# SwiGLU feed-forward on one core: the transposing load of tokens 256-511 goes from SyncE's queue to ScalarE's, and the first up weights the other way

## The chip, the core and the metric

The kernel runs on one core of a Trainium2 chip. The metric is the device time of one execution in microseconds (us), lower is better. The core has five engines with a queue of instructions each: TensorE (PE in the profile; PEld is its weight loader), VectorE (DVE), ScalarE (ACT), GpSimd (POOL) and SyncE (SP). SyncE only issues transfers here. Transfers that SyncE and ScalarE issue are moved by the same 16 DMA engines.

## The reference

```python
B, S, D, F = 1, 2048, 512, 1376
# x: (1, S, D); w_gate, w_up: (D, F); w_down: (F, D); all bf16

def reference(x, w_gate, w_up, w_down):
    g = _silu(x @ w_gate)
    u = x @ w_up
    return (g * u) @ w_down
```

## The kernel before, in words

**Stages.** TensorE contracts over the partitions, so x is needed transposed: `xT_sb` holds D in four blocks of 128 partitions, tokens along the free side. The 2048 tokens make four chunks of 512 (`c`), the 1376 columns of F ten blocks of 128 (`ft`) and 96 more. First stage: for each chunk and each `ft` a gate group and an up group, each of four matmuls (one for every block of D) into a PSUM bank; ScalarE applies SiLU to the gate bank, VectorE multiplies it with the up bank into `hT_sb`. The last 96 columns are made in groups X and Y. Second stage: the 16 token tiles times the down weights; VectorE copies each out (ScalarE one piece), SyncE stores it.

**The order of the first chunk.** The order of TensorE's work is written out by hand. It starts with eight matmuls on ones (`warm`, L337), which need no data. Then it waits for tokens 0-255, which are loaded as they lie (`xn_sb`, load "xn"), and transposes them itself: eight transposes into four banks (L346), two for each half of the tokens and each half of D. VectorE copies the two banks of D's first half to `xT_sb` (L293), ScalarE those of the second half (L280). Tokens 256-511 come by a transposing DMA instead (load "x0b", `load_x`, L87), as do tokens 512 to 2047 (x1, x2, x3).

So as not to wait for x0b, TensorE takes the first two gate and up groups in halves (L349-356): gate 0, up 0, gate 1, up 1 for tokens 0-255 first, then all four for tokens 256-511. Each waits, by `need`, for its own weights ("wg0", "wu0", "wg1", "wu1") and for the copies it reads; the second halves wait for x0b. From `ft` 2 on, a group has one matmul of 512 tokens for each block of D.

**Loads.** `load_w` (L91) brings a slab of columns of one weight; the slabs are block 0, block 1, blocks 2-3, 4-6, and 7 on. ScalarE issues gate 0 and up 0 (L104); behind these, in its own queue, come the table load with a dummy SiLU (L269), then the copies and SiLUs in the order of TensorE's groups (L270-280). SyncE issues all else (L107): xn, gate 1, up 1, x0b, the later slabs, the up tail ("wut"), x1 to x3, the down weights, and then it waits for each finished tile and stores it. In every queue the instructions run in order: an issue that takes long holds what stands behind it.

Of the kernel before, what the change touches and what calls it, by code (L numbers as in the profile page):

```python
# [13 lines left out]
def bass_standalone__swiglu_ffn__prompt_kernel(nc, x, w_gate, w_up, w_down, out):  # L14
    _, S, D = x.shape
    F = w_gate.shape[1]
    P = 128
# [4 lines left out]
    SC = 512  # L22
# [6 lines left out]
    HT = SC // 2  # L29
# [10 lines left out]
    UPH = F + 32  # L40
# [4 lines left out]
    with ExitStack() as es:  # L45
# [29 lines left out]
        loads = {}  # L75

        def load_sem(name):
            loads[name] = sem(f"s_{name}")
            return loads[name]
# [6 lines left out]
        def load_x(eng, name, t0, t1):  # L86
            eng.dma_start_transpose(  # L87
                xT_sb[:, :, t0:t1], xf[t0:t1, :]
            ).then_inc(load_sem(name), 16)

        def load_w(eng, name, src, base, f0, f1):  # L91
            eng.dma_start(
                w_sb[:, :, base + f0:base + f1],
                src[:, f0:f1].rearrange("(k p) f -> p k f", p=P),
            ).then_inc(load_sem(name), 16)

        slabs = [(0, 1), (1, 2), (2, 4), (4, 7), (7, NFT)]
        slab_of = {ft: a for a, b in slabs for ft in range(a, b)}

        def load_slab(eng, a, b):  # L100
            load_w(eng, f"wg{a}", w_gate, 0, a * P, min(b * P, F))
            load_w(eng, f"wu{a}", w_up, UPH, a * P, min(b * P, F - 32))

        def loads_on_scalar(act):  # L104
            load_slab(act, *slabs[0])

        def loads_on_sync(sp):  # L107
            sp.dma_start(
                xn_sb[:, :, :].rearrange("p j d -> p (j d)"), xf[0:HT, :].rearrange("(p j) d -> p (j d)", j=NXN)
            ).then_inc(load_sem("xn"), 16)  # L110
            load_slab(sp, *slabs[1])
            load_x(sp, "x0b", HT, SC)
            for a, b in slabs[2:]:
                load_slab(sp, a, b)
            load_w(sp, "wut", w_up, F - (F - 32), F - 32, F)
            for c in range(1, NSC):
                load_x(sp, f"x{c}", c * SC, (c + 1) * SC)
            sp.dma_start(
                wd_sb[:, 0:NFF, :], w_down[0:NFF * P, :].rearrange("(k p) d -> p k d", p=P)
            ).then_inc(load_sem("wd"), 16)  # L120
            for c in range(NSC):
                sp.dma_start(
                    wdt_sb[R * c:R * (c + 1), :, :], w_down[NFF * P:F, :].rearrange("(q p) d -> p q d", p=R)
                ).then_inc(load_sem(f"wdt{c}"), 16)
            sp.dma_start(wdl_sb[:, :], w_down[NFF * P:F, LASTA:D]).then_inc(load_sem("wdl"), 16)
# [123 lines left out]
        def rows_of(t):  # L249
            if t < NXN:  # L250
                return of[0:HT, :].rearrange("(p j) d -> j p d", j=NXN)[t]
            return of[t * P:(t + 1) * P, :]

        def on_sync(sp):
            loads_on_sync(sp)
            for t, c0, c1, ob, eng, n in stores:
                sp.wait_ge(s_A if eng == "A" else s_D, n)
                sp.dma_start(rows_of(t)[:, c0:c1], o_sb[ob][:, c0:c1]).then_inc(s_out[ob], 16)
            for i in range(NOS):
                sp.wait_ge(s_out[i], 16 * n_store[i])  # L260

        def on_gpsimd(pool):
            pool.iota(
                diag[:, :], pattern=[[-1, P]], base=0, channel_multiplier=1,
            ).then_inc(s_I, 1)

        def on_scalar(act):
            loads_on_scalar(act)
            act.activation(adummy[:, 0:4], zero_c, ACT.Silu)  # L269
            for op in act_ops:  # L270
                act.wait_ge(s_P, op["g"]["at"] + 1)
                if op["kind"] == "silu":
                    if op["free"]:
                        act.wait_ge(s_D, op["free"])
                    fn = ACT.Silu
                else:
                    if op["stored"][1]:
                        act.wait_ge(*op["stored"])
                    fn = ACT.Copy
                act.activation(op["out"], op["src"], fn).then_inc(s_A, 1)  # L280
# [15 lines left out]
        def on_tensor(pe):  # L296
# [136 lines left out]
                skip_group_check=True,  # L433
            ).then_inc(s_P, 1)

        on_sync(nc.sync)
        on_gpsimd(nc.gpsimd)
        on_scalar(nc.scalar)
        on_tensor(nc.tensor)
        on_vector(nc.vector)  # L440

# [27 lines left out]
```

## Time and profile before

| what | value |
|---|---|
| median of 3 runs | 120.66 us (120.31, 120.93, 120.66) |
| the profiled execution | 120.32 us; its span, first to last instruction, 118.9 us |
| granted TensorE clock | 1.00 |
| issue of x0b on SyncE | at 2.21 us, takes 1.69 us, landed at 6.38 us |
| issue of up 0 on ScalarE | at 1.22 us, takes 0.53 us, landed at 4.88 us |
| issues of x1, x2, x3 on SyncE | 4.54, 2.98, 1.80 us, from 8.86 us on |

The page of the profile gives busy times, the span in 40 slices of 3.0 us, the DMA queues, the chain of work that ended last, the costliest groups of instructions by line, and the transfers. Beside it stand answers of the trace: a timeline, the waits, the landings. In such lines "L87" is a line of the kernel, "out<-in" its tensors, "ACTq" and "SPq" the queues of ScalarE and SyncE while they issue a transfer, "x2" how many instructions; "[0.94 <-PE bank L346]" is idle time before and what ended it. All times in a timeline count from the first instruction of the span.

### The profile page before, as it was taken

How to read it: one execution, taken by the hardware profiler on the slowest of the kernel's cores; microseconds unless marked ns; L12 is line 12 of the kernel's file. 1: busy time of each engine (PE TensorE's matmuls, PEld its weight loads, DVE VectorE, ACT ScalarE, POOL GpSimd, SP SyncE). 2: the span in 40 equal slices, each digit the busy share in tenths (PEclk: the TensorE clock that was granted, in tenths of full speed). 3: DMA queues.
4: the chain of work that ended last, by engine and by line, in shares of the span. 5: the costliest groups of instructions: out<-in, count | busy, mean ns of one | idle time of the engine just before them, and what ended most of it. 6: DMA issues, size and time to landing. Idle time of an engine off the chain costs nothing.

```text
span 118.9 us, 1519 instructions
## 1 busy us (share of the span) xinstructions
PE 115.4 (97%) x600; PEld 54.1 (45%) x611; DVE 47.3 (40%) x73; ACT 31.0 (26%) x53; POOL 0.4 (0%) x5
## 2 busy tenths in 40 slices
PE   7999999999999999999999999999999999999993
PEld 2774444444444444444444444344434444444452
DVE  0133443353443444433444334469617422006530
ACT  4344324454234363244262343230000000000001
POOL 1000000000000000000000000000000000000000
PEclk9999999999999999999999999999999999999999
DMA  3999999970000000000000000000004221002412
GB/s 103 271 307 357 264 162 242 328 183 24 0 0 0 6 0 0 0 3 3 0 0 0 6 0 0 0 0 0 0 0 138 88 88 44 0 0 75 145 50 88
DMA packets 17559, 8.84 MB, mean 74 GB/s; under 512 B 10640, under 2 KB 17424, under 8 KB 17552
## 3 DMA queue, kind: packets, MB, share of 16 engines
q1 hardware_dynamic: 16496, 8.48, 26.7%
q10 hardware_dynamic: 1056, 0.26, 1.0%
q8 instruction: 5, 0.08, 0.3%
q14 instruction: 2, 0.02, 0.1%
HBM read 4.81 MB, written 2.10 MB: 58 GB/s over the span
## 4 chain that ended last, share of the span: by engine, by line
PE 97%; issue 1%; DVE 0%
PE bank L328 58%; PE bank L394 29%; PE bank L370 3%; PE bank L337 2%; PE bank L408 2%; PE bank L381 2%; PE bank L346 1%; DVE o_sb L293 0%; PE bank L431 0%
## 5 line engine op out<-in xcount | busy, mean ns | idle before, releaser
L328 PE MATMUL bank<-xT_sb,w_sb 128*128 128x512 bf16 (+2 forms) x338 | 69.7, 364 | 0.4
L328 PEld LDWEIGHTS bank<-xT_sb,w_sb 128*128 128x128 bf16 x344 | 32.8, 98 | 36.4 <-issue 0.2
L289 DVE TENSOR_TENSOR hT_sb<-sg_sb,bank 128x512 bf16<-128x512 f32 x40 | 27.5, 688 | 40.5 <-PE bank L328 36.6
L394 PE MATMUL bank<-wd_sb,hT_sb 128*128 128x512 bf16 (+2 forms) x166 | 34.5, 366 | 0.4 <-issue 0.3
L280 ACT ACTIVATE sg_sb<-bank 128x512 f32<-128x512 f32 x40 | 23.8, 596 | 40.8 <-PE bank L328 40.8
L394 PEld LDWEIGHTS bank<-wd_sb,hT_sb 128*128 128x128 bf16 x170 | 16.1, 98 | 19.1 <-issue 1.3
L293 DVE CAST o_sb<-bank 128x512 bf16<-128x512 f32 (+1 forms) x16 | 10.1, 663 | 22.0 <-PE bank L408 12.3
L280 ACT ACTIVATE o_sb<-bank 128x384 bf16<-128x384 f32 x1 | 0.5, 492 | 37.8 <-PE bank L394 37.8
L289 DVE TENSOR_TENSOR ht_sb<-sgy_sb,bank 32x512 bf16<-32x512 f32 x8 | 5.5, 684 | 0.2
L289 DVE TENSOR_TENSOR ht_sb<-sgx_sb,bank 32x512 bf16<-32x512 f32 x4 | 2.8, 691 | 3.5 <-ACT sgx_sb L280 3.5
L370 PE MATMUL bank<-xT_sb,w_sb 128*128 128x512 bf16 x15 | 4.1, 379 | 0.1
L337 PE MATMUL bank<-const-bfloat16-1.0 128*128 128x512 bf16 (+1 forms) x8 | 2.9, 545 | 0.8 <-PEq L454 0.8
L280 ACT ACTIVATE sgx_sb<-bank 32x512 f32<-32x512 f32 x4 | 2.4, 588 | 4.5 <-PE bank L370 4.5
L408 PE MATMUL bank<-wdt_sb,ht_sb 32*128 32x512 bf16 (+1 forms) x48 | 2.9, 372 | 0.0
L370 PEld LDWEIGHTS bank<-xT_sb,w_sb 128*128 128x128 bf16 x16 | 1.6, 98 | 1.9
L280 ACT ACTIVATE sgy_sb<-bank 64x512 f32<-64x512 f32 x4 | 2.4, 590 | 0.1
L337 PEld LDWEIGHTS bank<-const-bfloat16-1.0 128*128 128x128 bf16 x8 | 1.0, 136 | 2.4 <-issue 2.4
L381 PE MATMUL bank<-xT_sb,w_sb 128*64 128x512 bf16 x16 | 1.9, 382 | 0.0
L408 PEld LDWEIGHTS bank<-wdt_sb,ht_sb 32*128 32x128 bf16 x48 | 1.1, 93 | 1.7 <-issue 0.8
L269 ACT ACT_TABLE_LOAD x1 | 1.3, 1283 | 1.8 <-issue 1.8
L293 DVE COPY xT_sb<-bank 128x256 bf16<-128x256 bf16 x2 | 0.6, 292 | 2.7 <-PE bank L346 2.7
L381 PEld LDWEIGHTS bank<-xT_sb,w_sb 128*64 128x64 bf16 x16 | 0.8, 109 | 1.0 <-DVE hT_sb L289 0.4
(14 smaller groups left out, 4.0 us busy)
## 6 DMA issues: line engine op xcount, KB each, us to landing
out_dram<-o_sb SPq DMA_DIRECT2D x15, 128.0 KB, 1.7
wd_sb<-in_w_down_dram SPq DMA_DIRECT2D x1, 1280.0 KB, 9.2
w_sb<-in_w_gate_dram SPq DMA_DIRECT2D x1, 480.0 KB, 5.9
w_sb<-in_w_up_dram SPq DMA_DIRECT2D x1, 448.0 KB, 6.5
w_sb<-in_w_gate_dram SPq DMA_DIRECT2D x1, 384.0 KB, 4.5
w_sb<-in_w_up_dram SPq DMA_DIRECT2D x1, 384.0 KB, 5.1
wdt_sb<-in_w_down_dram SPq DMA_DIRECT2D x4, 96.0 KB, 7.5
xn_sb<-in_x_dram SPq DMA_DIRECT2D x1, 256.0 KB, 2.8
```

What stands on the lines that cost most here:

```text
L269: act.activation(adummy[:, 0:4], zero_c, ACT.Silu)
L280: act.activation(op["out"], op["src"], fn).then_inc(s_A, 1)
L289: ins = dve.tensor_tensor(op["out"], op["a"], op["b"], ALU.mult)
L293: ins = dve.tensor_copy(op["out"], op["src"])
L328: ins = pe.matmul(g["bank"][:, n0:n1], lhsT=w_sb[:, dk, col:col + P], rhs=xT_sb[:, dk, c * SC + n0:c * SC + n1], start=(dk == 0), stop=(dk ...
L337: pe.matmul(banks[NB - 1][:, 0:width], lhsT=ones_w, rhs=ones_m[:, 0:width], start=True, stop=True)
L346: ins = pe.transpose(tview(g["bank"])[:, k, :], xn_sb[:, g["i"], dk * P:(dk + 1) * P], ident[:, :])
L370: ins = pe.matmul(g["bank"][:, :], lhsT=w_sb[:, dk, XC0:XC0 + P], rhs=xT_sb[:, dk, c * SC:(c + 1) * SC], start=(dk == 0), stop=(dk == KD - 1),
L381: ins = pe.matmul(g["bank"][y0:y1, :], lhsT=w_sb[:, dk, YC0:YC0 + 64], rhs=xT_sb[:, dk, c * SC:(c + 1) * SC], start=(dk == 0), stop=(dk == ...
L394: ins = pe.matmul(g["bank"][:, 0:c1 - c0], lhsT=hT_sb[:, fk, t * P:(t + 1) * P], rhs=wd_sb[:, fk, c0:c1], start=(start and fk == 0), stop= ...
L408: ins = pe.matmul(g["bank"][:, 0:c1 - c0], lhsT=ht_sb[R * c:R * (c + 1), q, j * P:(j + 1) * P], rhs=wdt_sb[R * c:R * (c + 1), q, c0:c1], s ...
```

## The change

ScalarE issues gate 0 and then x0b, the transposing load. SyncE issues xn, then up 0, gate 1, up 1 and the later slabs, each in the place that is now free, and x0b is no longer among them. Ahead of x1, the first transposing load that SyncE still has, it waits until x0b has landed, so that transposing loads of the two queues are never in flight together. The last hunk only has ScalarE's instructions emitted ahead of SyncE's, since the semaphore of x0b is made where x0b is issued.

```diff
         def loads_on_scalar(act):
-            load_slab(act, *slabs[0])
+            load_w(act, "wg0", w_gate, 0, 0, P)
+            load_x(act, "x0b", HT, SC)
 
         def loads_on_sync(sp):
             sp.dma_start(
                 xn_sb[:, :, :].rearrange("p j d -> p (j d)"), xf[0:HT, :].rearrange("(p j) d -> p (j d)", j=NXN)
             ).then_inc(load_sem("xn"), 16)
+            load_w(sp, "wu0", w_up, UPH, 0, P)
             load_slab(sp, *slabs[1])
-            load_x(sp, "x0b", HT, SC)
             for a, b in slabs[2:]:
                 load_slab(sp, a, b)
             load_w(sp, "wut", w_up, F - (F - 32), F - 32, F)
+            sp.wait_ge(loads["x0b"], 16)
             for c in range(1, NSC):
                 load_x(sp, f"x{c}", c * SC, (c + 1) * SC)
...
+        on_scalar(nc.scalar)
         on_sync(nc.sync)
         on_gpsimd(nc.gpsimd)
-        on_scalar(nc.scalar)
         on_tensor(nc.tensor)
         on_vector(nc.vector)
```

## The prediction

> **What bounds the kernel now.** First the busy times and the slices (page, parts 1 and 2).
>
> ```profile
> PE 115.4 (97%) x600; PEld 54.1 (45%) x611; DVE 47.3 (40%) x73; ACT 31.0 (26%) x53; POOL 0.4 (0%) x5
> ...
> DMA  3999999970000000000000000000004221002412
> ```
>
> TensorE is busy for 115.4 us of the 118.9 us span; the transfers fill the first quarter only. A change that touches loads can move the time only where TensorE waits for a load. So second the chain of waits, in order of time (start, duration, what), at its beginning:
>
> ```profile
> 0.77 2.93 PE bank L337 x8
> 3.71 0.70 PE bank L346 x8
> 4.41 0.07 issue
> 4.47 3.87 PE bank L328 x40
> 8.35 0.05 issue
> 8.40 10.74 PE bank L328 x49
> ```
>
> L337 are the matmuls on ones that fill the wait for x, L346 the eight TensorE transposes of tokens 0-255, L328 the gate and up matmuls. From 4.47 us on the chain is matmul after matmul. Whatever the change brings is decided before about 8.4 us; only the loads needed there count. Third the waits between 4 and 9 us (total, times, longest):
>
> ```profile
> ACT xT_sb L280 <- PE bank L346: 0.9, 1, 0.9
> PEld bank L328 <- issue: 0.2, 1, 0.2
> PEld bank L328 <- DMA xT_sb<-in_x_dram: 0.2, 1, 0.2
> ```
>
> The load that moves, the transposing load of tokens 256-511 ("x0b" below), is the only load that TensorE is seen to wait for, 0.17 us by its weight loader. The matmul row shows less: the last first-half matmul starts at 6.266 us and its successors follow 0.109 us apart, so the next was due at 6.375 and came at 6.426: **0.05 us**. That is all that this wait can give back. ScalarE meanwhile waits 0.9 us before its first copy of transposed x. Fourth, the timeline at the start (start, duration):
>
> ```profile
> 1.22 0.53 ACTq L92 DMA_DIRECT2D w_sb<-in_w_up_dram  x1
> ...
> 1.78 1.28 ACT L269 ACT_TABLE_LOAD   x1 [1.78 <-issue]
> 2.20 1.69 SPq L87 DMA_TRANSPOSE xT_sb<-in_x_dram  x1
> ...
> 3.08 0.20 ACT L269 ACTIVATE act_dummy<-const-float32-0.0 128x4 f32<-128x4 f32 x1
> ...
> 4.22 0.66 ACT L280 ACTIVATE xT_sb<-bank 128x256 bf16<-128x256 bf16 x2 [0.94 <-PE bank L346]
> ```
>
> The transposing load holds its issuing engine for 1.69 us, an ordinary load for about 0.5. And ScalarE, on which it now goes, has its table load, its dummy SiLU and the copies of L280 behind its loads.
>
> **Part 1: ScalarE's order.** Removed there: issue of up 0, 0.531 us from 1.223. Added there: issue of x0b, of unknown length d on this engine. Nearest row: the same load on SyncE, 1.690. Lower end: the load of tokens 1536-2047 has twice the tokens and took 1.795, so half of it is 0.90. Upper end: that of tokens 512-1023, behind a full queue, took 4.537. I take 1.69, same size and same neighbours. Then: 1.223 + 1.690 = 2.913 issue done; + 0.03 gap + 1.283 table load = 4.23; + 0.01 + 0.205 dummy = 4.44; the first copy starts near **4.46** in place of 4.221. The cover is the 0.9 us wait above, and it ends at d = 1.47 (2.75 + d = 4.22). In other words 1.16 us of added hold lie against 0.92 us of cover, and **0.24 us** show. TensorE is behind it at once: its third matmul waits for this copy now too (second at 4.530, third at 4.660 instead of 4.586), and four matmuls later for the second copy (0.04 us late). Both copies shift together, so the delay counts once: +0.24. VectorE's copies (4.04, 4.33) do not move.
>
> The Trainium skill, page "ScalarE: Activation LUTs", section "What ACT_TABLE_LOAD costs", adds a drain of about 1.38 us to the 1.283 us of the load itself. The trace shows no such drain: the dummy starts 0.01 us behind the load. With it the copies would be 1.38 us later still, about 122.3 us for the median; I give that 1 in 100, within the slow rival below.
>
> **Part 2: the transfers.** Landings now, issue plus time to landing (page, part 6):
>
> ```profile
> xn_sb<-in_x_dram SPq DMA_DIRECT2D x1, 256.0 KB, 2.8
> ...
> w_sb<-in_w_gate_dram ACTq DMA_DIRECT2D x1, 128.0 KB, 3.2
> w_sb<-in_w_gate_dram SPq DMA_DIRECT2D x1, 128.0 KB, 3.4
> w_sb<-in_w_up_dram ACTq DMA_DIRECT2D x1, 128.0 KB, 3.7
> w_sb<-in_w_up_dram SPq DMA_DIRECT2D x1, 128.0 KB, 3.7
> ```
>
> x lands at 3.50, gate 0 at 3.93 (needed at 4.44), gate 1 at 4.58 (5.45), up 0 at 4.88 (5.00), up 1 at 5.33 (5.83), x0b at 6.38 (6.37). All but x move as packets of 256 B: 512 for each weight, 1024 for x0b. By the trace's packet records the DMA engines are full from 2 us on (share 0.96 or more in each stretch to 6.5 us), and between 3.5 and 5.5 us start 2218 such packets, 1109 a us; the last of the 3072 starts near 5.75. While both queues had packets (3.5 to 4.5 us) SyncE's moved 596 and ScalarE's 517: about half each.
>
> After the change gate 0 and x are as before, since the second load of each queue stands behind its first: x lands at 3.5, gate 0 at 3.9. At 3.5 us x0b follows gate 0 in ScalarE's queue, and SyncE's has up 0 (383 packets left), gate 1, up 1. At 555 packets a us each, up 0 ends at 4.19, gate 1 at 5.11 with 129 of x0b left, x0b at 5.34, up 1 at 5.69. From last packet to landing the trace has 0.4 to 0.5 us for weights (0.48 gate 1, 0.55 up 1) and 0.62 for x0b. So up 0 lands near 4.6 (earlier than now), gate 1 at 5.6 (needed at 5.45 + 0.24 = 5.69), x0b at 5.96, and **up 1 at 6.24**, needed at 5.83 + 0.24 = 6.07. Up 1 takes x0b's place as the late load: its four half-width matmuls run from about 6.29 to 6.73, where the second halves now start at 6.43: +0.30. If SyncE's queue is served first, up 1 is in time and the end of Part 1 alone counts: 6.375 + 0.24 = 6.615, or +0.19. Part 1 lies inside Part 2's delay, they do not add.
>
> What speaks against any gain here is a rule of the Trainium skill, "DMA: Bandwidth & Descriptors", section "Issuing engines are not separate DMA queues": loads from several engines share the same 16 DMA engines, and a second issuer saves only issue time. By it up 1 is late as worked out (+0.30); if x0b had engines of its own, the +0.19 would remain. The packet counts above side with the rule.
>
> **Part 3: the rest of SyncE's queue.** Later weights are issued 1.2 us earlier, but their packets stand behind the same 3072 as before, so gate 2-3 still lands near 7.2, needed at 8.08 + 0.25: no cost. The new wait on x0b comes on SyncE after the up tail (7 issues at about 0.55 from 2.75, then 1.44: near 7.5 us); x0b has landed at 5.96, so it does not hold. Queued behind it are the loads of tokens 512 on, the down weights and the stores. Tokens 512-1023 land at 17.0 now and are needed at 23.0: 6 us of cover, and if the wait held, it would have to hold that long to cost anything. Emitting ScalarE's program ahead of SyncE's moves no instruction on any engine: 0.
>
> **Sum.** +0.19 to +0.30; I take +0.25. Against the profiled execution (120.32, span 118.9 and 1.4 around it) 120.57; that run is at the low end of the three shown, so against their median of 120.66 I forecast **120.91 us**. Half a per cent, 0.6 us, is about what a measurement of this kernel can tell from no change: this is no change.
>
> **Rivals.**
> *x0b was the late load more often than the profile shows.* It has no slack now, and the runs shown spread from 120.31 to 120.93; if the upper ones wait longer for it, a landing at 5.96 takes that wait away. With d under 1.47 and SyncE's queue served first, this gives -0.05 in the profiled run and up to -0.35 in the median: 120.3 to 120.6. For it: the lower end of d, 0.90. Against: the full DMA engines. Chance 0.17, of which 0.05 under 120.06.
> *Slower: ScalarE is held longer.* The place is the first copy at L280; it pays from d = 1.47, us for us, and passes half a per cent at d near 2.1. With the 2.976 us that the load of tokens 1024-1535 held SyncE, it is 0.24 + 1.29 - 0.05 = +1.5, or 122.1. For it: two of four such loads took that or more. Against: those stood behind long queues, here only gate 0 stands ahead. Chance 0.15, most of it over the bound.
> *SyncE's issues wait for ScalarE's transposing issue.* Then gate 1 is issued near 2.9, lands 3.4 later at 6.3 against 5.69 (+0.6), and up 1 3.7 behind 3.4, at 7.1 against 6.7 (+0.3): +0.9 beside the 0.24, or 121.8. Against: the issues at 1.20 and 1.22 on the two engines run side by side in 0.41 and 0.53. Chance 0.08.
> The forecast has 0.55; 0.05 is for what I do not see.
>
> **Numbers.** Faster: 0.05 + 0.03 unnamed = 0.08. Slower: 0.12 of ScalarE held, 0.08 of SyncE held, 0.02 unnamed = 0.22. Same: the rest, 0.70. The range goes from the first rival's low end, 120.3, to the SyncE rival's time, 121.8; outside are d beyond 2.6 and the unnamed.
>
> **What would show it.** Right: an x0b issue row on ACTq of about 1.7 us from 1.22, the first L280 copy near 4.46, no wait of L328 for x0b, a wait for w_sb (up 1) of 0.2 us near 6.2, and the chain from 8.4 on as before but 0.25 later. Wrong: that copy still at 4.22 with up 1 landing by 5.8; or ACTq's row over 2.1 us; or SyncE rows for gate 1 or up 1 well over 0.5 us.

## The result and the profile after

The changed kernel takes 121.09 us, median of 20 runs (120.82 to 121.55), against 120.64 us (120.30 to 121.20, 20 runs): ratio 1.004, 95% interval 1.0027 to 1.0053. That is 0.45 us slower. The profiled execution took 121.06 us with a span of 119.6 us.

Busy times and slices of the changed kernel; line numbers are two higher than before, L330 for L328 and so on:

```profile
PE 115.7 (97%) x600; PEld 54.3 (45%) x611; DVE 47.2 (39%) x73; ACT 31.0 (26%) x53; POOL 0.4 (0%) x5
...
DMA  2999999940000000000000000000003221002412
```

TensorE's work is the same; a wait has come on top. The chain at its beginning (start, duration, what) names it:

```profile
1.20 0.41 SPq L92
1.61 0.05 issue
1.66 4.56 DMA w_sb<-in_w_gate_dram
6.22 0.05 issue
6.27 2.79 PE bank L330 x24
```

Before, the chain was matmuls from 0.77 us on. Now it is the load of gate 1, issued by SyncE at 1.66 and landed at 6.22, 4.56 us later; the same load took 3.4 before. The waits between 4 and 9 us (total, times, longest):

```profile
PEld bank L330 <- DMA w_sb<-in_w_gate_dram: 0.6, 1, 0.6
PE bank L330 <- DMA w_sb<-in_w_gate_dram: 0.4, 1, 0.4
```

The wait for x0b is gone, a wait for gate 1 stands in its place: the matmul due at 5.68 starts at 6.27, 0.59 us late. The timeline shows the new order of issue, and that ScalarE is not the cause:

```profile
1.20 0.41 SPq L92 DMA_DIRECT2D w_sb<-in_w_up_dram  x1
1.24 1.30 ACTq L87 DMA_TRANSPOSE xT_sb<-in_x_dram  x1
...
1.66 0.50 SPq L92 DMA_DIRECT2D w_sb<-in_w_gate_dram  x1
...
2.20 0.51 SPq L92 DMA_DIRECT2D w_sb<-in_w_up_dram  x1
...
2.58 1.28 ACT L271 ACT_TABLE_LOAD   x1 [2.58 <-issue]
...
3.87 0.20 ACT L271 ACTIVATE act_dummy<-const-float32-0.0 128x4 f32<-128x4 f32 x1
...
4.38 0.68 ACT L282 ACTIVATE xT_sb<-bank 128x256 bf16<-128x256 bf16 x2 [0.30 <-PE bank L348]
```

x0b holds ScalarE for 1.30 us. ScalarE is done with its dummy at 4.08 and waits 0.30 us for TensorE's transposes, so its hold is still covered.

**One number for all kernels.** Call T the start of the first matmul that reads x0b's tokens (the second half of gate 0). Span minus T is 112.48 to 112.50 us in 11 of the 14 profiles of this study: behind T nothing changes, and a kernel is as late as its T. T was 6.42 in the profile of before and 7.15 after. The other three have a wait or a slower clock behind T, told below.

| kernel | gate 1 landed | up 1 landed | x0b issued by, at | x0b landed | T | ratio to before (95%) |
|---|---|---|---|---|---|---|
| before | 4.58 | 5.33 | SyncE 2.20 | 6.38 | 6.42 | |
| before, again | 4.68 | 5.40 | SyncE 2.20 | 6.40 | 6.84 | |
| emission order only | 4.56 | 5.40 | SyncE 2.20 | 6.57 | 6.72 | 0.9995 (0.9978 to 1.0011) |
| after | 6.22 | 6.59 | ScalarE 1.24 | 6.34 | 7.15 | 1.0040 (1.0027 to 1.0053) |
| after, again | 6.47 | 6.87 | ScalarE 1.23 | 6.64 | 7.40 | |
| x0b behind the dummy | 6.46 | 6.96 | ScalarE 1.29 | 6.72 | 7.45 | 1.0049 (1.0030 to 1.0068) |
| x0b in two | 5.96 | 6.53 | ScalarE 1.23, 2.53 | 7.95 | 8.08 | 1.0164 (1.0124 to 1.0204) |
| plain load in its place | 5.65 | 6.23 | SyncE 2.75 | 7.18 | 7.32 | 1.0044 (1.0029 to 1.0058) |
| x0b first on SyncE | 6.07 | 6.49 | SyncE 1.20 | 5.61 | 7.00 | 1.0017 (1.0001 to 1.0034) |
| gate 1 on ScalarE | 4.91 | 5.79 | ScalarE 1.86 | 9.64 | 9.69 | 1.0183 (1.0145 to 1.0220) |
| x0b issued last | 5.94 | 6.80 | ScalarE 2.76 | 10.81 | 10.86 | 1.0417 (1.0368 to 1.0467) |
| x0b issued last, alone | 5.49 | 6.04 | ScalarE 2.76 | 6.98 | 7.02 | 1.0117 (1.0084 to 1.0150) |
| plain load issued last | 5.86 | 7.15 | SyncE 2.76 | 8.46 | 8.51 | 1.0131 (1.0104 to 1.0158) |
| mirror image | 4.63 | 5.55 | SyncE 2.21 | 9.30 | 9.35 | 1.0255 (1.0214 to 1.0297) |

All times are in us from the start of the span, each from one profile. The ratios compare fast executions alone, and the profile of "gate 1 on ScalarE" is of one of its two slow ones (125.27 us; its four fast ones took 122.18 to 123.33), so its x0b and T are later than its ratio has them.

**Why gate 1 is late.** The packet records of the changed kernel, packets of 256 B started in each quarter of a microsecond:

| from, us | 3.50 | 3.75 | 4.00 | 4.25 | 4.50 | 4.75 | 5.00 | 5.25 |
|---|---|---|---|---|---|---|---|---|
| SyncE's queue | 188 | 229 | 65 | 0 | 36 | 125 | 209 | 261 |
| ScalarE's queue | 89 | 51 | 215 | 281 | 248 | 154 | 71 | 4 |

SyncE's packets up to 4.25 are up 0's. Then x0b has the DMA engines nearly to itself, and gate 1's packets begin in earnest at 4.75, 3.1 us behind their issue. The first theory was: **packets of both queues reach the DMA engines in the order of issue**, and gate 1 was issued 0.43 us behind x0b. The rivals: equal shares, as I had forecast; or a transposing load on one queue keeps the other queue's packets off.

### The profile page after: what moved, and what is told of

The parts are those of the page before. It is cut to its first block, busy times and chain, and to the rows that moved or that the text cites. A ratio compares the mean times of both kernels' runs of the same rounds, so it can differ in the third digit from the quotient of the medians.

```text
span 119.6 us, 1519 instructions
## 1 busy us (share of the span) xinstructions
PE 115.7 (97%) x600; PEld 54.3 (45%) x611; DVE 47.2 (39%) x73; ACT 31.0 (26%) x53; POOL 0.4 (0%) x5
## 4 chain that ended last, share of the span: by engine, by line
PE 93%; DMA 4%; issue 1%; SPq 1%; DVE 0%
PE bank L330 57%; PE bank L396 29%; DMA w_sb<-in_w_gate_dram 4%; PE bank L372 3%; PE bank L410 2%; PE bank L383 2%; SPq L92 0%; SPq L109 0%; DVE o_sb L295 0%; PE bank L433 0%
## 5 line engine op out<-in xcount | busy, mean ns | idle before, releaser
L330 PE MATMUL bank<-xT_sb,w_sb 128*128 128x512 bf16 (+2 forms) x338 | 69.8, 364 | 0.7 <-DMA w_sb<-in_w_gate_dram 0.4
L330 PEld LDWEIGHTS bank<-xT_sb,w_sb 128*128 128x128 bf16 x344 | 32.9, 98 | 36.8 <-DMA w_sb<-in_w_gate_dram 0.6
```

Of the source, the lines that this page charges most:

```text
L330: ins = pe.matmul(g["bank"][:, n0:n1], lhsT=w_sb[:, dk, col:col + P], rhs=xT_sb[:, dk, c * SC + n0:c * SC + n1], start=(dk == 0), stop=(dk ...
```

## The experiments

**Emission order alone.** The kernel before with one part of the change:

```diff
+        on_scalar(nc.scalar)
         on_sync(nc.sync)
         on_gpsimd(nc.gpsimd)
-        on_scalar(nc.scalar)
```

> The kernel before with ScalarE's instructions emitted ahead of SyncE's and nothing else. All theories: within 0.15 us of before, the same landings. If x itself lands 0.13 us later here as it did in the changed kernel's profile, the emission order would carry that part of the loss.

Ratio 0.9995, all landings near those of before: the emission order does nothing that can be measured. x landed at 3.58 here, at 3.49 and 3.52 in the two profiles of before, at 3.60 (x0b first on SyncE) and 3.66 (mirror image) in two kernels below, at 3.62 and 3.70 in those of the changed kernel: the 0.13 us by which x was later in the profile after lies within the spread over these kernels.

**x0b behind the dummy SiLU in ScalarE's queue.**

```diff
-            load_x(act, "x0b", HT, SC)
...
             act.activation(adummy[:, 0:4], zero_c, ACT.Silu)
+            load_x(act, "x0b", HT, SC)
```

> As the changed kernel, but ScalarE issues x0b behind its table load and dummy SiLU, so near 2.75 us instead of 1.24, and SyncE has issued gate 1 (1.66) and up 1 (2.21) ahead of it. Theory A, issue order: the packets of a transposing load issued on one engine go to the DMA engines ahead of a load that the other engine issues later, so gate 1 (issued 0.43 us behind x0b in the changed kernel) was kept off the wire by x0b's 1024 packets. Then here gate 1 lands by 4.9 us and up 1 by 5.5, the wait of TensorE for gate 1 (0.59 us) is gone, x0b lands at 6.2 to 6.6, and the time is within 0.2 us of before. Theory B, equal shares: the two queues alternate packet by packet; gate 1 lands near 5.0, up 1 near 5.6, since x0b joins later; time as in A. Theory C, a transposing load on the other queue keeps SyncE's packets off the wire whenever it runs: up 1 or gate 2-3 stops for about 0.9 us while x0b's packets run, seen as a gap in the 256-byte or 512-byte packets of SyncE's queue; a wait of 0.3 us or more for up 1 if x0b's packets start before 4.5 us.

It did not do what it was made for. ScalarE's lines:

```profile
1.23 1.28 ACT L270 ACT_TABLE_LOAD   x1 [1.23 <-PEq L456]
1.29 1.31 ACTq L87 DMA_TRANSPOSE xT_sb<-in_x_dram  x1
...
4.20 0.66 ACT L282 ACTIVATE xT_sb<-bank 128x256 bf16<-128x256 bf16 x2 [1.46 <-PE bank L348]
```

The issue ran beside the table load, at 1.29, not behind it: an issue holds what stands behind it in ScalarE's queue, but it did not itself wait for the table load and the dummy ahead of it. So x0b was issued only 0.06 us later, and gate 1 landed at 6.46 again. What the run does show: ScalarE now waits 1.46 us in front of its copies, its hold is gone altogether, and the kernel is as slow as the changed one. The hold of ScalarE costs nothing here.

**x0b in two halves of 128 tokens.**

```diff
-            load_x(act, "x0b", HT, SC)
+            load_x(act, "x0b", HT, HT + P)
+            load_x(act, "x0c", HT + P, SC)
```

(SyncE and TensorE wait for both.)

> As the changed kernel, but x0b is two transposing loads of 128 tokens, one behind the other on ScalarE (512 packets each). Theory A, issue order: the first half is issued at 1.24, gate 1 at 1.66, the second half near 1.95, so gate 1 has only the first half ahead of it and lands about 0.45 us earlier than in the changed kernel, near 5.75; TensorE's wait for it falls from 0.59 to about 0.15 us. Theory B, equal shares: gate 1 near 5.6 as forecast, with or without the cut. Theory C, a transposing load of the other queue keeps SyncE's packets off: no change, gate 1 lands at 6.2 and the wait is 0.6 us. ScalarE is held some 0.3 us longer (two issues), which can make its first copy up to 0.2 us late.

Gate 1 landed at 5.96, 0.26 to 0.51 us earlier than in the two profiles of the changed kernel: fewer packets ahead of it, as the order of issue has it, though 5.75 was expected. TensorE did not wait for gate 1. The price was elsewhere: each half held ScalarE as long as the whole (1.27 and 1.29 us), and now the cover was used up:

```profile
1.23 2.59 ACTq L87 DMA_TRANSPOSE xT_sb<-in_x_dram  x2
3.85 1.28 ACT L273 ACT_TABLE_LOAD   x1 [3.85 <-issue]
...
5.26 0.64 ACT L284 ACTIVATE xT_sb<-bank 128x256 bf16<-128x256 bf16 x2
```

The first copy starts at 5.26, and TensorE waits 1.0 us for it by its weight loader. This is the mechanism of Part 1 of the prediction, with twice the hold. A second wait follows: the second half, issued at 2.53, landed at 7.95, and the matmul due at 7.39 started at 8.08.

**A plain load in x0b's place.**

```diff
         def loads_on_scalar(act):
-            load_x(act, "x0b", HT, SC)
+            load_w(act, "wg2", w_gate, 0, 2 * P, 4 * P)
...
             load_slab(sp, *slabs[1])
+            load_x(sp, "x0b", HT, SC)
```

(SyncE then issues up 2-3 and the rest; no wait for x0b.)

> As the changed kernel, but in x0b's place ScalarE issues an ordinary load of 256 KB, the gate weights of blocks 2-3 (512 packets of 512 B), and SyncE issues x0b behind up 1. It tells whether the transposing load is special. Theory A in its plain form (any load issued earlier goes first): gate 1 and up 1 are behind those 256 KB, gate 1 lands near 6.0 and TensorE waits for it 0.3 us or more. If only transposing loads go first: the two queues alternate as up 0 and gate 1 did before, gate 1 lands near 5.2 to 5.4 and up 1 near 5.8, with no wait for gate 1. In either case x0b comes last, near 7 us, and TensorE waits for it about 0.5 us, so the time is 0.4 to 0.7 us over before.

Gate 1 landed at 5.65, between the two forecasts (6.0 and 5.2 to 5.4). From 4.0 to 4.5 us ScalarE's queue started 268 packets, SyncE's 111: the load issued earlier leads here too, so the order does not need a transposing load. Equal shares from the start, the first rival, fails in both kernels. The expected wait for x0b did not come in this profile: it landed at 7.18, and TensorE, whose matmuls had run at half their pace until near 6.8, reached it only at 7.32. Here T is TensorE's pace, so this kernel's ratio need not be the cost of its loads.

**x0b first on SyncE: order without the second queue.** The kernel before, one line moved:

```diff
+            load_x(sp, "x0b", HT, SC)
             load_slab(sp, *slabs[1])
-            load_x(sp, "x0b", HT, SC)
```

> The kernel before with one line moved: SyncE issues x0b ahead of gate 1 and up 1. ScalarE is as before (gate 0, up 0). Issue order: gate 1 and up 1 stand behind x0b without any second queue; gate 1 lands at 6.2 or later, TensorE waits for it 0.5 us or more, the second halves start at 7.1 to 7.4, and the loss is that of the changed kernel or more, +0.4 to +0.8 us. If the loss comes from x0b being on ScalarE's queue: gate 1 is late here too since one queue is in order, so this run tells only whether order alone is enough for the whole loss.

Its wait for a load between 4 and 12 us:

```profile
PEld bank L328 <- DMA w_sb<-in_w_gate_dram: 0.3, 1, 0.3
```

The same wait for gate 1 with no queue changed, so order alone brings the kind of loss; it is smaller than expected (1.0017 against 1.0040; the intervals just overlap, 1.0034 and 1.0027). Gate 1, issued at 2.57 behind all of x0b in one queue, landed at 6.07; in the changed kernel, issued at 1.66 in the other queue, at 6.22 and 6.47. The packet records say what the two have in common. Of the 3072 packets of 256 B, gate 1's last is the 2561st to start here, the 2562nd and 2560th in the two profiles of the changed kernel, and was the 1325th before. So one queue or two, the order puts gate 1 at the same place. It started at 5.43 here, at 5.39 in the first profile after: there the changed kernel is later only behind its last packet, which took 0.83 us to land, against 0.64 here and 0.46 before. Why the landing took longer, no run shows.

**Gate 1 ahead of x0b on ScalarE.**

```diff
         def loads_on_scalar(act):
-            load_x(act, "x0b", HT, SC)
+            load_w(act, "wg1", w_gate, 0, P, 2 * P)
...
             act.activation(adummy[:, 0:4], zero_c, ACT.Silu)
+            load_x(act, "x0b", HT, SC)
```

(SyncE: x, up 0, up 1, the later slabs.)

> As the changed kernel, but gate 1 goes to ScalarE ahead of x0b: ScalarE gate 0, gate 1, x0b (behind the dummy in the queue, so that the table load runs beside the issue), SyncE x, up 0, up 1, later weights. Issue order: gate 1 and up 0 are issued together at 1.2, up 1 at 1.66, x0b at 1.75 or a little later: gate 1 lands by 4.9, up 1 shares with x0b and lands at 5.3 to 6.2, x0b at 6.2 to 6.6; the second halves start at 6.4 to 6.8, the time is within 0.25 us of before. Transposing load preferred: up 1 lands only with x0b's last packets or after, 6.4 or later, second halves at 7.0, time +0.4 us.

The order part came as expected: gate 1 at 4.91, up 1 at 5.79, no wait for either. But x0b landed at 9.64 in place of 6.2 to 6.6, and TensorE's weight loader waited 3.5 us for it. From 5.5 to 6.5 us SyncE's packets of 512 B and x0b's of 256 B started 60 to 88, 69 to 79, 78 to 87, 74 to 80 in the quarters. So here, with packets of both queues there, they start in near equal numbers, but both are slow: together 229 GB/s, and 102 from 6.5 to 7.0, where the kernel before moved 285 from 3.5 to 4.5 with both queues. By the Trainium skill, page "DMA: Bandwidth & Descriptors", section "Queues, rings and completion order", each DMA engine goes round between the queues packet by packet; these counts agree.

**x0b issued last, by a wait.**

```diff
-            act.activation(adummy[:, 0:4], zero_c, ACT.Silu)
+            act.activation(adummy[:, 0:4], zero_c, ACT.Silu).then_inc(s_W, 1)
+            act.wait_ge(s_W, 1)
+            load_x(act, "x0b", HT, SC)
```

> As the changed kernel, but ScalarE issues x0b only when its table load and dummy SiLU are done, by a wait on a semaphore of the dummy's own; near 2.75 us, so behind SyncE's issues of gate 1 (1.66) and up 1 (2.21). (The run with x0b behind the dummy in the queue but without a wait issued x0b at 1.30 beside the table load, so it did not test this.) Issue order: packets of both queues reach the DMA engines in the order of issue; gate 1 lands by 5.2, up 1 by 5.6, x0b at 6.3 to 6.7; TensorE does not wait for gate 1; the second halves of the first four groups start at 6.4 to 6.8 and the time is within 0.2 us of before. Transposing load or ScalarE's queue preferred: gate 1 or up 1 still lands after 5.9, the second halves start at 7.0 or later, and the time stays 0.4 us or more over before.

A clear miss of every theory: x0b, issued at 2.76, landed at 10.81. In windows (busy time and count of each engine, granted clock, DMA share, GB/s):

```profile
4.00:5.50 1.50, 1.39 (x23) 1.11 (x20) 0.55 (x2) 0.66 (x2) 0.00 (x0) 1.00 0.86 161
5.50:7.00 1.50, 0.90 (x9) 0.45 (x7) 0.00 (x0) 0.00 (x0) 0.00 (x0) 1.00 1.14 242
7.00:8.00 1.00, 0.46 (x4) 0.16 (x2) 0.00 (x0) 0.00 (x0) 0.00 (x0) 1.00 1.32 34
```

From 7 to 8 us the DMA engines are as busy as at full speed (1.32, where 1.28 is usual) and move 34 GB/s. Their packets last long: x0b's 256 B took 165 ns on average from 7.00 to 7.25 and 282 ns in the next quarter, against 18 ns at full speed.

The new theory: **interference**. A transposing load and ordinary loads of the other queue that have packets in flight at the same time slow each other. Three runs for it.

**The mirror image.** The kernel before, x0b in its old place on SyncE, ordinary loads on ScalarE beside it:

```diff
             act.activation(adummy[:, 0:4], zero_c, ACT.Silu)
+            load_slab(act, *slabs[2])
...
-            for a, b in slabs[2:]:
+            for a, b in slabs[3:]:
                 load_slab(sp, a, b)
```

> The mirror image: the kernel before, with x0b on SyncE as third of its loads, but ScalarE issues the ordinary loads of gate 2-3 and up 2-3 behind up 0 (near 1.8 to 2.9 us, beside its table load), so that they are in flight on ScalarE's queue while x0b's packets run on SyncE's. Interference (a transposing load and ordinary loads of the other queue slow each other while both have packets in flight, whichever engine issues which): x0b's packets take over 25 ns on average where they take 18 to 20 ns in the kernel before, x0b lands at 7.2 us or later (6.38 before), and the time is 0.5 us or more over before. If it is ScalarE's queue that is bad for a transposing load, and not the mixture: packets stay at 18 to 20 ns, x0b lands by 7.1 (1024 more packets of 512 B share the engines), and the time is 0 to 0.6 us over before.

x0b landed at 9.30. Windows of this kernel (columns as above), and below them of the kernel with x0b first on SyncE, where from 5.0 to 5.5 only SyncE's queue has packets:

```profile
5.50:6.50 1.00, 1.00 (x11) 0.97 (x10) 0.00 (x0) 0.00 (x0) 0.00 (x0) 1.00 1.41 167
6.50:7.50 1.00, 1.00 (x9) 0.64 (x6) 0.00 (x0) 0.00 (x0) 0.00 (x0) 1.00 0.98 190
```

```profile
5.00:5.50 0.50, 0.50 (x9) 0.42 (x8) 0.00 (x0) 0.17 (x1) 0.00 (x0) 1.00 1.28 283
```

167 and 190 GB/s in the mixture against 283 in one queue. From 5.5 to 6.5 us x0b's packets took 25 to 78 ns on average in each quarter, the longest 568. The extra packets alone explain less: had both loads run at their usual speed (1024 packets at 1109 a us, 1024 of 512 B at some 670 a us as between 6.25 and 7.0 in the changed kernel), all would have been through 2.4 us after 4.75, and x0b landed by 7.8. So the slowing is not peculiar to a transposing load that ScalarE issues.

**x0b issued last, alone.** As issued last, but SyncE waits for x0b ahead of blocks 2-3:

```diff
             load_slab(sp, *slabs[1])
+            sp.wait_ge(loads["x0b"], 16)
             for a, b in slabs[2:]:
                 load_slab(sp, a, b)
             load_w(sp, "wut", w_up, F - (F - 32), F - 32, F)
-            sp.wait_ge(loads["x0b"], 16)
```

> As the run with x0b issued last by ScalarE behind a wait, but SyncE also waits for x0b before it issues blocks 2-3 and all later loads, so that x0b shares the DMA engines with the ends of gate 1 and up 1 only. It parts the order of issue from the mixture. Interference: with little to mix with, gate 1 lands by 5.3, up 1 by 5.8, x0b by 6.8, its packets at 18 to 22 ns; the second halves start at 6.4 to 6.9. If a transposing load that ScalarE issues at 2.76 is slow by itself: x0b lands at 8 us or later as in that run (10.8). In both cases gate 2-3 is issued only after x0b landed and comes about 3 us later, so TensorE waits for it (about 1.5 us) and the whole is 1 to 3 us slower than before; the landings are what is compared.

x0b landed at 6.98 in place of 10.81, gate 1 at 5.49, up 1 at 6.04, each 0.2 us later than expected, and TensorE waited for none of the three. With nothing of SyncE's behind it, the transposing load from ScalarE is as fast as it was from SyncE (4.2 us from issue to landing in both). Its packets were not all at the 18 to 22 ns expected: while the last of up 1's were in flight, from 5.25 to 5.75, they took 53 and 43 ns on average in the two quarters. That the kernel is still slower is the wait for gate 2-3, 1.1 us, which this edit makes; span minus T has the same 1.1 us on top.

**The control: a plain load issued last.**

```diff
-            load_x(act, "x0b", HT, SC)
+            load_w(act, "wg2", w_gate, 0, 2 * P, 4 * P)
...
             load_slab(sp, *slabs[1])
+            load_x(sp, "x0b", HT, SC)
```

(On the kernel with x0b issued last, with its wait for the dummy; SyncE then issues up 2-3 and the rest.)

> The control of the run with x0b issued last: the same wait on ScalarE, but what it then issues near 2.76 us is the ordinary load of gate 2-3 (256 KB), and SyncE issues x0b behind up 1. Interference needs a transposing load on one queue and ordinary ones on the other; here gate 2-3's packets meet gate 1's and up 1's, both ordinary. Expected: gate 1 lands by 5.3, up 1 by 5.8, packets at 18 ns (256 B) and 27 to 30 ns (512 B) until x0b's start; x0b then meets the end of gate 2-3 and may be slowed a little: 7.0 to 8.0. If two queues in flight were slow whatever they carry: gate 1 lands at 5.9 or later, as with x0b in this place (5.95).

A mixed answer. From 5.25 to 6.25 us both queues moved 294 GB/s, nearly all in ordinary packets; x0b's joined at 6.0, and from 6.25 on the rate was less than half:

```profile
4.00:5.25 1.25, 1.25 (x15) 0.99 (x13) 0.58 (x2) 0.77 (x2) 0.00 (x0) 1.00 0.88 170
5.25:6.25 1.00, 1.00 (x12) 1.00 (x11) 0.00 (x0) 0.00 (x0) 0.00 (x0) 1.00 1.10 294
6.25:7.25 1.00, 0.83 (x7) 0.42 (x5) 0.00 (x0) 0.00 (x0) 0.00 (x0) 1.00 1.36 133
```

That speaks for interference. But gate 1 landed at 5.86, not by 5.3, and up 1 at 7.15, not by 5.8: from 4.00 to 5.25 the DMA engines were short of packets (share 0.88, where 1.22 to 1.28 is usual), as they were with x0b issued last (0.86), before any of x0b's packets had started. In both kernels ScalarE and SyncE issue at the same moment, 2.76, behind a full SyncE queue; alone at that moment (the run before this one) the share was 1.22. Gate 1's last packet, started at 4.68, also took 1.18 us to land, against 0.46 in the kernel before. Which of this does it stays open.

**Both kernels a second time.**

> The changed kernel unchanged, a second profile. Expected: gate 1 lands at 6.0 to 6.5 again, ScalarE's issue of x0b takes 1.25 to 1.35 us, and the span is 118.92 us plus what the start of the second halves is later than the 6.43 us of the profile of before, within 0.05 us.

> The kernel before unchanged, a second profile. Expected: the span is 118.92 us plus what the start of the second halves is later than 6.43 us, within 0.05 us; x0b lands at 6.3 to 6.7; where the span is longer than 118.92, the 128-column matmuls keep their 0.107 us spacing for longer (to 4.01 us in the first profile, 5.4 us in the run with only the order of emission changed).

After: gate 1 at 6.47, issue 1.31 us, span 119.89 = 112.49 + 7.40. Before: x0b at 6.40, span 119.32 = 112.48 + 6.84. In this second profile of before TensorE did not wait for x0b at all: its 128-column matmuls stood 0.107 us apart until 5.74 us, where they went to 0.056 from 4.01 on in the first profile. So a usual run of before is later by TensorE's own pace, not by a load: by the same offsets the median of 120.64 has T near 6.8.

## Why the prediction was right, and where not

The time lies in the range and on the side forecast, within half a per cent: +0.45 us where +0.25 was forecast, above its bounds of +0.19 to +0.30. That it came so near is partly luck. Between the two profiles T moved by 0.73 us, over twice the +0.30 that was the most of its sum. The medians lie only 0.45 apart because most runs of before are later than its profile, by TensorE's own pace as far as the second profile and that of the emission order show; the prediction did not have this. Step by step:

- **What bounds the kernel**: right. Everything is decided before T.
- **Part 1, ScalarE's hold**: mis-sized, and as a result not there. d was 1.30 us, not 1.69; the cover ends at 1.47. What was missing is the place in the queue: second in its queue x0b held the issuing engine 1.30 us on ScalarE and 1.31 on SyncE (x0b first on SyncE), third on ScalarE 1.64 (gate 1 on ScalarE), fourth on SyncE 1.69 to 1.83, fifth 1.86 and 2.37 (the two kernels with a plain load in its place). The lower end of 0.90, by halving, was no bound either: 128 tokens took 1.27. The +0.24 did not occur; the run with the dummy ahead showed that ScalarE's hold is worth nothing here, the run in two halves that beyond the cover it costs what the formula says (2.59 us of issue; the first copy at 5.34 by the formula, measured at 5.26; TensorE 1.0 us late).
- **Part 2, the transfers**: the mechanism was right (x0b takes the wire from the weights and one of them becomes the late load), the step "x0b in ScalarE's queue and gate 1 and up 1 in SyncE's move at 555 packets a us each" failed. Up 0 landed at 4.52 (forecast 4.6), but gate 1's packets were not there when up 0's ended: x0b, issued 0.43 us ahead of gate 1, led. Gate 1 landed at 6.22 (forecast 5.6), and it, not up 1, was the late load: a wait of 0.59 us against the forecast 0.2 for up 1. Up 1 landed at 6.59 when it was due at 6.72. x0b landed at 6.34 (5.96), due at 7.15. One reading was off without effect: in the profile of before x0b's last packet starts at 5.87, not near 5.75, so it landed 0.51 us behind it, not 0.62.
- **Part 3**: right. SyncE reached x1 at 8.14, and x0b had landed at 6.34; no wait; gate 2-3 landed at 7.33, needed at 8.79.
- **The rule of the Trainium skill against a gain** ("DMA: Bandwidth & Descriptors", "Issuing engines are not separate DMA queues") held: nothing was gained. The measurements go beyond it: the place among all loads changed, which cost time, and in several kernels here packets of the two queues slowed each other.
- **The rivals**: that x0b is the late load of before more often than its profile shows did not appear; in none of the three profiles with before's order does TensorE wait for it more than 0.05 us. ScalarE held longer and SyncE's issues held: neither occurred (1.30 us; 0.41, 0.50 and 0.51 us for SyncE's rows beside it).
- **The sum against the profile**: the profile of before is at the low end of its runs. TensorE's late pace and the wait for gate 1 lie side by side, so a run that is late by its pace loses less to the load.

How much of the 0.45 us is order and how much interference is only roughly settled. Order alone, in one queue, cost 0.2 us (0.01 to 0.41). In the first profile of the changed kernel nothing else slowed the packets while x0b and gate 1 shared the DMA engines (columns as in the windows above):

```profile
4.50:5.00 0.50, 0.50 (x9) 0.32 (x6) 0.29 (x1) 0.50 (x2) 0.00 (x0) 1.00 1.27 288
5.00:5.50 0.50, 0.50 (x11) 0.43 (x9) 0.00 (x0) 0.05 (x1) 0.00 (x0) 1.00 1.28 279
```

So the wait of 0.59 us in that profile is order, and the longer landing. In its second profile the same mixture moved 230 GB/s from 4.5 to 5.25 us, with packets of up to 26 ns on average in a quarter, and with x0b behind the dummy 181, with up to 32; gate 1's last packet then started at 5.56 and 5.69 in place of 5.39. So by that start interference adds from nothing to 0.3 us here, and it differs between executions. Why the mixture is slow, and why not always, no run shows. Long packets also occur without a transposing load in flight: with x0b issued last, alone, the first packets of gate 2-3 (8.0 to 8.5 us) took 58 ns on average, and 27 later. None of the versions was faster than before.

## What to carry to other kernels

Moving a load to another queue moves its place among all loads. Write down, by issue time over both queues, what will stand ahead of what, and compare with the order in which the compute engine needs it: here x0b, needed last, went ahead of gate 1 and up 1. Keep a transposing load in one queue with the loads around it, or leave the other queue empty while it runs: three further kernels here that did neither lost 2.2 to 5.0 us. And compare a cover with a second profile: the wait of 0.05 us that the change could remove was not there in the other two profiles with before's order of loads.

## What the hardware showed unexpectedly

- A transposing load mixed with ordinary loads of the other queue: 34 to 190 GB/s at DMA shares of 0.98 to 1.41 in three kernels, where one queue moves about 285 at 1.28; but 279 to 288 at 1.27 and 1.28 in the first profile of the changed kernel.
- A transposing issue takes 1.27 to 1.31 us, for 128 tokens as for 256, when it is second in its queue (the second load of 128, third, took 1.29).
- A DMA issue that stands behind a table load and an activation in ScalarE's queue runs beside them (1.29 to 2.60, the table load 1.23 to 2.52).
- At the start the profile shows a granted clock of 1.00 while 128-column matmuls still stand 0.107 us apart; the full speed (0.056) came before 3.7 us at one end (gate 1 on ScalarE) and near 6.8 at the other (plain load in its place), with the same start at 0.77. Behind a long idle it shows the slow clock: with x0b issued last TensorE idled over 3 us in front of T, and the 16 second halves behind it stood 0.21 us apart instead of 0.109, at a granted clock of 0.50 from 10.86 to 14.2 us. In the kernel with gate 1 on ScalarE, which idled as long, it was 0.50 from 10.3 to 13.7; these two have 1.6 and 1.7 us more behind T than the others. The Trainium skill, page "TensorE: Matmul & The Clock Gate", Part 1, gives the array half its clock until it has been busy for about 3.4 us, and again after an idle window of that length, at a moment that differs from run to run; the 3.4 us at 0.50 and the full speed 2.9 to 6.0 us after the first matmul agree with it roughly. The chain of waits of the kernel with x0b issued last:

```profile
2.76 8.05 DMA xT_sb<-in_x_dram
...
10.86 3.53 PE bank L332 x16
```
